# A retention layer and a gated convolution on one core: the lead-in in a new order and on other banks, the loads of the loop issued later

## The chip, the core and the metric

The kernel runs on one core of a Trainium2 chip. The core has a matrix engine (TensorE, "PE" in the profile, with its weight loads as "PEld"), VectorE ("DVE"), ScalarE ("ACT"), GpSimd ("POOL") and a queue engine (SyncE, "SP") that issues most DMAs. Each engine takes its instructions strictly in the order of the program and waits at semaphores for the others. The metric is the device time of one execution in microseconds (us).

## What is computed

For 8 sequences of 576 rows with 8 heads of 64, a causal retention (scores with a decay per head, no softmax) is followed by a gated linear unit whose gate is a causal convolution of 5 taps:

```python
scores = (q @ k.T) / sqrt(64)
ret    = scores * gamma[h] ** (row - col)   # 0 where col > row
x      = ret @ v                            # heads side by side: [8, 576, 512]
gate   = sigmoid(sum_k conv_w[k] * x shifted by 4 - k rows)
out    = ((gate * (x @ w_val)) @ w_out)     # float32, [8, 576, 512]
```

Inputs and output are float32; the kernel multiplies in bfloat16.

## The kernel before

**Units.** A unit is 256 rows of one sequence (two 128-row chunks), so units 0 to 15 are the two halves of the eight sequences. Units 16 and 17 hold the last 64 rows of four sequences each. The order of work on every engine is written out by hand (`tc.manual_schedule()`), unit by unit, and Tile only adds the semaphores.

**What happens to a unit.** `load_half` (L104) brings half the heads of k, q or v, 256 KB, over the SP queue (L113); units 0, 1, 16 and 17 are loaded whole, the last two in four pieces per tensor (L97). Many loads have a *touch*: a one-element copy on DVE or ACT into the tile (L112), for which the DMA waits, so the touch's place in that engine's order sets when the DMA goes out. `cast1` and `cast_half` (L256, L274) convert to bf16; v is always converted on POOL (L264, L282), k and q on POOL or another engine. `turn` (L296) or, in the loop, `turn_halves` (L306) transposes k and q on PE, and `take_part` (L321) or L319 copies the result to `kqt`. `scores` multiplies them, `masks` (L346) applies the causal mask on DVE. `values` multiplies the masked scores with v into the banks `o0` and `o1`; `carried` adds the contribution of earlier rows from a running state to the same banks. `update` multiplies k with v, ACT copies the product to `xf` (L453, L455) and `states` (L464) adds it to the state on POOL. `take_x` (L414) scales the result on DVE into `xg`. Then `conv` and `gates` (the sigmoid on ACT, L527), `value` and `gated` (DVE, L547), and `project` with its copy on ACT (L562) and `store`.

**Order.** The stretch from the start to about 43 us, here called the lead-in, is a list of such calls without a loop: it takes units 0 to 3, loads the weights, and leaves every unit at its place in the pipeline. The loop `for n in range(4, NU)` (L770) then runs 14 turns. Turn n does `carried`, the second half of `scores`, and `values` of unit n, `conv`, `value` and `project` of unit n-1, and `update`, `turn_halves` and casts of the units ahead. POOL gets in turn n, in this order: the states of unit n+1, v of n+2, the second halves of k and q of n+2, and the first halves of k and q of n+3; the transposes that need these first halves stand in turn n+1.

**Banks.** PSUM has the pools `ps_a` (one tile of two banks), `ps_s` (one of two), `ps_o` (`o0`, `o1`) and `ps_v` (two tiles of one bank). A new tile waits for the last reader of the old one in its place.

**Fillers.** `warm(n, cols)` multiplies a zero tile. `fill()` (L151) adds zero products until the count of matmuls at the start of the loop has the remainder 50 modulo 127.

```python
def load_half(n, u, i, touch=None):
    ...
    if touch:
        touch(t[0:1, 0, 0:1], lsc[0:1])
    nc.sync.dma_start(out=t, in_=...)
```

All matmuls and transposes are recorded under L146, so groups of PE are told apart by their tiles.

Of the kernel before, what the change touches and what calls it, by code (L numbers as in the profile page):

```python
# [21 lines left out]
def kernel(  # L22
# [10 lines left out]
    nc = tc.nc  # L33
# [44 lines left out]
    with tc.manual_schedule():  # L78
# [72 lines left out]
        def fill():  # L151
            z = ps_v.tile([P, 512], F32, name="v")
            while (made[0] + 4 * NP) % BLOCK != PLACE:
                matmul(z[:, 0:64], lhsT=zero[:, 0:P], rhs=zero[:, 0:64], start=True, stop=True)
# [80 lines left out]
        def prep_wv(e, eng):  # L235
            for (j0, ab, hl) in (((0, 0, 0), (64, 0, 1)), ((0, 1, 1), (64, 1, 0)))[e]:
                for pr in range(2):
                    eng(wvb[e][:, :, pr, j0:j0 + 64], wvf[2 * pr + ab][:, :, hl * 64:hl * 64 + 64])

        def prep_wo(os, eng):  # L240
            for o in os:
                if o < 2:
                    eng(wob[:, o, :], wof[o])  # L243
                else:
                    eng(wob[lo, o, :], wof[o][hi])
                    eng(wob[hi, o, :], wof[o][lo])

# [57 lines left out]

        def turn_halves(*pairs):  # L306
            if len(pairs) == 1:
                ps = ps_v.tile([P, 1, 2, 2, 2, P], BF16, name="v")
            else:
                ps = ps_a.tile([P, 2, 2, 2, 2, P], BF16, name="a")  # L310
            for (at, (u, hf)) in enumerate(pairs):
                for i in range(2):
                    for prl in range(2):
                        for r in range(2):
                            h = 2 * (2 * hf + prl)
                            transpose(ps[:, at, i, prl, r, :], bf[u]["kq"[i]][:, r, h:h + 2, :].rearrange("p h d -> p (h d)"), ident)
            for (at, (u, hf)) in enumerate(pairs):
                new_turned(u)
                nc.scalar.copy(kqt[u][hf].rearrange("p i l r c a -> p (i l r c a)"), ps[:, at].rearrange("p i l r a -> p (i l r a)"))  # L319

        def take_part(u, i, eng):  # L321
            for hf in range(2):
                eng(kqt[u][hf][:, i].rearrange("p l r c a -> p (l r c a)"),  # L323
                    tps[u, i][:, hf].rearrange("p l r a -> p (l r a)"))
# [49 lines left out]
        def carried(u, odd, chs=(0, 1)):  # L374

            kind, b, cu = units[u]
            o = out_banks(u)
            for pr in range(NP):
                t = kqt[u][pr // 2]
                for c in chs:  # L380
                    par = c ^ odd
# [16 lines left out]
        def fence(u, rows, c, eng=None):  # L398
            t = small.tile([P, 1], F32, name="fence", bufs=2)
            (eng or nc.scalar.copy)(t[rows], ops[u][c][rows, NP - 1, 0:1])  # L400

        def values(u, hf):
# [29 lines left out]

        def update(u, own=False, now=True):
            kind, b, cu = units[u]
# [3 lines left out]
            if own:  # L438
                xy = [ps_v.tile([P, 512], F32, name="v") for c in range(2)]
            else:  # L440
                xyt = ps_s.tile([P, 2, 512], F32, name="s")
                xy = [xyt[:, c] for c in range(2)]
# [20 lines left out]

        def states(u):  # L464
            kind, b, cu = units[u]
# [10 lines left out]
            else:  # L476
                mid = stp.tile([P, NP, 64], F32, name="mid")
                nc.gpsimd.tensor_tensor(mid, state[b, "run"], xf[:, 0], op=ALU.add)  # L478
                nc.gpsimd.tensor_copy(s1, mid)
                s2 = stp.tile([P, NP, 64], BF16, name=f"s4{b}", bufs=1)  # L480
                nc.gpsimd.tensor_tensor(s2, mid, xf[:, 1], op=ALU.add)
            state[b, 2 * cu + 1] = s1
            state[b, 2 * cu + 2] = s2

# [60 lines left out]
        def gated(j, i, e):  # L545
            ss = sets(j, i)
            nc.vector.tensor_tensor(zsb[j][:, 2 * e + ss[0]:2 * e + ss[-1] + 1, :], gsb[j, i][e], vps[j, i, e], op=ALU.mult)  # L547
# [81 lines left out]
        warm(2)  # L629
        update(0, own=True)  # L630
        cast1("q", 1, act)
        cast1("v", 1)
        values(0, 0)
        warm(1, 512, ps_s)
        values(0, 1)
        fence(0, lo, 1, dve)
        turn(1, ps_v, 0)
        take_part(1, 0, act)
        take_x(0, (0,))
        carried(0, 1)  # L640
        carried(0, 0)
        turn(1, ps_v, 1)
        take_x(0, (1,))
        take_part(1, 1, dve)
        conv(0, 0)
        load_wv(1, act)
        load_wv(3)
        carried(1, 1, (0,))
        carried(1, 0, (0,))
        scores(1, 0)  # L650
        masks(1, 0)
        load_half("k", 3, 0, dve)
        scores(1, 1, pool=ps_a)
        masks(1, 1)
        load_half("k", 3, 1, dve)
        cast1("k", 2)
        update(1, own=True)
        cast1("q", 2, act)
        load_half("q", 3, 0, act)
        cast1("v", 2)  # L660
        values(1, 0)
        turn(2, ps_v, 0)
        take_part(2, 0, act)
        warm(1, 512, ps_s)
        values(1, 1)
        take_x(1, (0,))
        fence(1, lo, 1, dve)
        load_half("q", 3, 1, dve)
        warm(2, 512, ps_s)
        turn(2, ps_v, 1)  # L670
        take_part(2, 1, dve)
        load_half("v", 3, 0, dve)
        carried(1, 1, (1,))
        carried(1, 0, (1,))
        take_x(1, (1,))
        load_half("v", 3, 1, dve)
        warm(1, 512, ps_s)
        scores(2, 0)
        masks(2, 0)
        load_wo(0, dve)  # L680
        load_wo(1)
        scores(2, 1, pool=ps_v)
        masks(2, 1)
        load_wo(2, dve)
        load_wo(3)
        prep_wv(0, pool)
        prep_wv(1, act)
        conv(1, 0)
        update(2)
        cast1("k", 3)  # L690
        values(2, 0)
        values(2, 1)
        take_x(2, (0,))
        fence(2, lo, 1, dve)
        load_half("k", 4, 0, dve)
        value(0, 0, 0)
        carried(2, 1)
        carried(2, 0)
        take_x(2, (1,))
        load_half("k", 4, 1, dve)  # L700
        gated(0, 0, 0)
        load_half("q", 4, 0, dve)
        gate_values(0, 1)
        load_half("q", 4, 1, dve)
        cast1("v", 3)
        cast1("q", 3, act)
        conv(2, 0)
        gate_values(1, 0)
        load_half("v", 4, 0, dve)
        load_half("v", 4, 1)  # L710
        gate_values(1, 1)
        load_half("k", 5, 0, dve)
        load_half("q", 5, 0)
        turn(3, ps_o, 0)
        take_part(3, 0, act)
        turn(3, ps_o, 1)
        take_part(3, 1, dve)
        update(3, now=False)
        states(3)
        prep_wo((0, 1), pool)  # L720
        prep_wo((2, 3), act)
        cast1("k", 4)
        gate_values(2, 0)
        load_half("v", 5, 0, dve)
        load_half("v", 5, 1)
        gate_values(2, 1)
        cast1("q", 4, act)
        cast1("v", 4)
        scores(3, 0)
        masks(3, 0)  # L730
        load_half("k", 5, 1, dve)
        load_half("q", 5, 1)
        carried(3, 0)
        scores(3, 1, lambda: carried(3, 1), pool=ps_a)
        masks(3, 1)
        load_half("k", 6, 0, dve)
        load_half("q", 6, 0)
        project(0, 0, 0, 4)
        project(0, 0, 1, 4)
        store(0)  # L740
        turn_halves((4, 0))
        project(1, 0, 0, 4)
        values(3, 1)
        values(3, 0)
        cast_half("k", 5, 0)
        cast_half("q", 5, 0)
        update(4)
        take_x(3)
        load_half("v", 6, 0, dve)
        load_half("v", 6, 1)  # L750
        turn_halves((4, 1), (5, 0))
        project(1, 0, 1, 4)
        store(1)
        scores(4, 0)
        masks(4, 0)
        prep_tail_mask()
        load_half("k", 6, 1, dve)
        load_half("q", 6, 1)
        cast1("v", 5)
# [4 lines left out]
        fill()  # L764
        project(2, 0, 0, 4)
        project(2, 0, 1, 4)
        store(2)
        load_half("k", 7, 0)
        load_half("q", 7, 0)
        for n in range(4, NU):  # L770
# [8 lines left out]
            conv(n - 1, 0)  # L779
            bring("v", n + 3, 0, act)  # L780
            if nxt:
                scores(n + 1, 0, pool=ps_v)
                masks(n + 1, 0)
                update(n + 1)
            bring("v", n + 3, 1, act)
            values(n, 1)
            values(n, 0)
            gate_values(n - 1, 0)
            bring("k", n + 3, 1, dve)
            gate_values(n - 1, 1)  # L790
            bring("q", n + 3, 1, dve)
            take_x(n, (0,))
            take_x(n, (1,))
            bring("k", n + 4, 0, dve)
            if n + 2 < NU:
# [6 lines left out]
            if nxt:  # L802
                turn_halves((n + 1, 1), *([(n + 2, 0)] if n + 2 < NU else []))
            bring("q", n + 4, 0, act)
            project(n - 1, 0, 0, 2)
# [36 lines left out]
```

## Time and profile before

| | |
|---|---|
| runs shown | 159.75, 160.12, 162.49 us (median 160.12) |
| the profiled execution | 159.02 us, span of the trace 157.3 us |
| granted TensorE clock | 0.999 |
| busy: PE, PEld | 145.8 us (93%), 115.3 us |
| busy: DVE, ACT, POOL | 105.2, 93.4, 102.4 us |
| moved by DMA | 40.37 MB, mean 257 GB/s |
| chain that ended last | PE 80%, DVE 8%, DMA 3%, ACT 2% |

The span is the time from the first to the last instruction of the program; the execution's own time is 1.7 us longer. In the timeline's rows, the first number is the start, the second the duration of the group, "xN" the number of instructions, and the bracket tells how long the engine stood idle before the group and who ended that. Matmuls overlap in the records, so the cost of a group of matmuls is read from its start to the start of the next one.

### The profile page before, as it was taken

To read this page: it belongs to the slowest core of one execution; us is meant where nothing else is said; L and a number is where in the kernel's file an instruction comes from. 1 tells how busy PE (TensorE), PEld (TensorE's weight loads), DVE (VectorE), ACT (ScalarE), POOL (GpSimd) and SP (SyncE) were. 2 spreads that over 40 slices of the span, in tenths; PEclk is the share of its full clock that TensorE was granted. 3 is DMA by queue.
4 is the path that set the end of the run, shared out by engine and by line. 5 is a ranking of instruction groups with operands and counts; after the bars stand their busy time and mean duration, and the time that the engine had idled before them with its cause. 6 is when DMAs were issued, how large, how long until landed. Compare 5 with 4: busy or idle time off the path is not lost.

```text
span 157.3 us, 8008 instructions
## 1 busy us (share of the span) xinstructions
PE 145.8 (93%) x3461; PEld 115.3 (73%) x3461; DVE 105.2 (67%) x214; ACT 93.4 (59%) x164; POOL 102.4 (65%) x166
## 2 busy tenths in 40 slices
PE   6977989989999999999999999999999999998960
PEld 2456667868788878877878788887878887876720
DVE  5786887693676867667768686767667676765340
ACT  6895664697846574747484848484656637252510
POOL 7679669397969695959596877869695842500000
PEclk9999999999999999999999999999999999999999
DMA  4999999999989999998999899899778872302135
GB/s 117 347 347 342 324 290 333 325 310 308 351 276 292 300 352 363 321 315 234 305 264 314 249 322 285 262 314 267 213 230 241 262 236 108 137 17 121 36 101 133
DMA packets 62561, 40.37 MB, mean 257 GB/s; under 512 B 2346, under 2 KB 59710, under 8 KB 62526
## 3 DMA queue, kind: packets, MB, share of 16 engines
q1 hardware_dynamic: 62400, 39.59, 82.1%
q8 instruction: 27, 0.44, 1.2%
q10 hardware_dynamic: 126, 0.27, 0.7%
q14 instruction: 8, 0.07, 0.1%
HBM read 30.42 MB, written 9.44 MB: 253 GB/s over the span
## 4 chain that ended last, share of the span: by engine, by line
PE 80%; DVE 8%; DMA 3%; ACT 2%; issue 1%; SPq 1%; POOL 1%; POOLq 0%; DVEq 0%
PE v L146 45%; PE a L146 19%; PE o L146 10%; PE s L146 7%; DVE p L356 3%; DMA fv<-in_v_dram 2%; DVE p L352 2%; SPq L586 1%; DMA out_dram<-ob 1%; DVE z L547 1%; DVE kq L323 1%; ACT ob L562 1%; POOL wob L243 1%; DVE xg L421 1%; ACT gate L527 1%
## 5 line engine op out<-in xcount | busy, mean ns | idle before, releaser
L319 ACT COPY kq<-a 128x1024 bf16<-128x1024 bf16 x26 | 25.0, 1015 | 28.0 <-PE a L146 28.0
L146 PE MATMUL v<-xg,wvb 128*128 128x256 bf16 x288 | 34.8, 273 | 0.3
L146 PE MATMUL v<-wob,z 128*128 128x256 bf16 (+1 forms) x209 | 32.9, 305 | 1.2 <-POOL wob L243 0.6
L547 DVE TENSOR_TENSOR z<-gate,v 128x512 bf16<-128x512 f32 x34 | 23.3, 686 | 14.0 <-PE v L146 11.5
L356 DVE TENSOR_TENSOR p<-s,mask 128x1024 bf16<-128x1024 f32 x17 | 20.8, 1223 | 17.1 <-PE s L146 17.1
L146 PEld LDWEIGHTS <-wvb 128*128 128x128 bf16 x288 | 26.7, 97 | 5.2 <-issue 0.2
L264 POOL TENSOR_TENSOR vb<-fv,gin 128x512 bf16<-128x512 f32 x28 | 28.6, 1042 | 0.0
L146 PEld LDWEIGHTS <-z 128*128 128x128 bf16 x217 | 20.3, 98 | 9.2 <-issue 1.7
L421 DVE TENSOR_TENSOR xg<-o,gout 128x512 bf16<-128x512 f32 x32 | 22.3, 736 | 4.5 <-PE o L146 4.4
L527 ACT ACTIVATE gate<-a 128x1024 f32<-128x1024 f32 x17 | 17.4, 1024 | 12.6 <-ACT ob L562 6.7
L146 PE MATMUL a<-xg,dg 64*64 64x256 bf16 x720 | 24.3, 270 | 0.6 <-DVE xg L421 0.3
L562 ACT COPY ob<-v 128x512 f32<-128x512 f32 x34 | 18.6, 581 | 5.1 <-PE v L146 5.1
L146 PEld LDWEIGHTS <-dg 64*64 64x64 bf16 x720 | 20.0, 106 | 1.4 <-issue 0.7
L146 PEld LDWEIGHTS <-kb 64*64 64x64 bf16 (+1 forms) x656 | 15.9, 107 | 5.0 <-DVE p L356 2.0
L271 POOL CAST kb<-fk 128x512 bf16<-128x512 f32 x28 | 17.0, 612 | 0.1
L146 PEld LDWEIGHTS <-kq 64*64 64x64 bf16 x576 | 15.6, 106 | 2.0 <-issue 1.7
L352 DVE TENSOR_TENSOR p<-v,mask 128x512 bf16<-128x512 f32 x24 | 15.4, 685 | 1.0
L478 POOL TENSOR_TENSOR mid<-run,xf 128x256 f32<-128x256 f32 x8 | 5.8, 726 | 13.5 <-ACT xf L455 12.3
L271 POOL CAST qb<-fq 128x512 bf16<-128x512 f32 x22 | 13.5, 614 | 0.1
L146 PE MATMUL o<-p,vb 64*64 64x128 bf16 x576 | 12.3, 218 | 0.9 <-DVE p L356 0.5
L146 PEld LDWEIGHTS <-s 64*64 64x64 bf16 x256 | 8.2, 107 | 6.2 <-issue 3.4
L146 PE MATMUL s<-kq 64*64 64x128 bf16 x304 | 12.2, 222 | 0.4 <-DVE kq L323 0.3
(98 smaller groups left out, 197.2 us busy)
## 6 DMA issues: line engine op xcount, KB each, us to landing
out_dram<-ob SPq DMA_DIRECT2D x16, 512.0 KB, 4.5
fk<-in_k_dram SPq DMA_DIRECT2D x28, 256.0 KB, 4.5
fq<-in_q_dram SPq DMA_DIRECT2D x28, 256.0 KB, 4.6
fv<-in_v_dram SPq DMA_DIRECT2D x28, 256.0 KB, 4.6
wkc<-in_k_dram SPq DMA_DIRECT2D x2, 512.0 KB, 5.0
wqc<-in_q_dram SPq DMA_DIRECT2D x2, 512.0 KB, 5.5
wvc<-in_v_dram SPq DMA_DIRECT2D x2, 512.0 KB, 5.9
wvf<-in_moe_w_val_dram SPq DMA_DIRECT2D x4, 256.0 KB, 4.9
```

The lines of the kernel that those rows point to most:

```text
L146: return f(*a, **k)
L243: eng(wob[:, o, :], wof[o])
L264: nc.gpsimd.tensor_tensor(b[n][:, hs].rearrange("p h r d -> p (h r) d"), f.rearrange("p h (r d) -> p (h r) d", r=2), gin[:, units[u][2], h ...
L271: (eng or nc.gpsimd.tensor_copy)(b[n][:, :, hs].rearrange("p r h d -> p h r d"), f.rearrange("p h (r d) -> p h r d", r=2))
L319: nc.scalar.copy(kqt[u][hf].rearrange("p i l r c a -> p (i l r c a)"), ps[:, at].rearrange("p i l r a -> p (i l r a)"))
L352: nc.vector.tensor_tensor(p[:, par].rearrange("p l r a -> p l (r a)"), sps[u, hf][par].rearrange("p l r a -> p l (r a)"), mrow.to_broadcas ...
L356: nc.vector.tensor_tensor(p.rearrange("p e l r a -> p (e l) (r a)"), sps[u, hf].rearrange("p e l r a -> p (e l) (r a)"), mrow.to_broadcast ...
L421: nc.vector.tensor_tensor(x[:, b, :, PAD + i0:PAD + i0 + P].rearrange("p o (a r) -> p o r a", r=2), o[c].rearrange("p o (r a) -> p o r a", ...
L478: nc.gpsimd.tensor_tensor(mid, state[b, "run"], xf[:, 0], op=ALU.add)
L527: nc.scalar.activation(t, cps[j, i], AF.Sigmoid)
L547: nc.vector.tensor_tensor(zsb[j][:, 2 * e + ss[0]:2 * e + ss[-1] + 1, :], gsb[j, i][e], vps[j, i, e], op=ALU.mult)
L562: (eng or nc.scalar.copy)(outs[u][:, r], o)
```

## The change

The lead-in's list of calls is rewritten from the first `update` to the loop, some calls go to other banks and engines, and in the loop every load stands three transfers later. In detail:

- `update(0)` takes `ps_s` in place of two tiles of `ps_v`, `update(1)` also `ps_s`, `update(3)` and `update(4)` take `ps_o`. `scores(1, 1)` takes `ps_v` in place of `ps_a`.
- `turn_both(3, ...)` puts the transposes of k and q of unit 3 into one tile of `ps_s`, ahead of both copies. `conv(0)` and `conv(1)` have their `gates` later in the order.
- The copies of the turned k parts of units 1 and 2 go from ACT to DVE, the q part of unit 1 from DVE to ACT; the casts of k and q of unit 3 and of parts of others go to ACT.
- `fence_zero(1)` and `fence_first(3)` are one-column DVE reads of the bank just written by `carried`, which `values` then waits for. `carried` runs its heads and chunks backwards.
- `states` can be cut in two (`states_last`).
- Of the zero products, `warm` of 64 columns x12 comes in, three calls of `warm` with 512 columns go out, and `fill()` aims at the same remainder with one `project` left behind it.
- In the loop, turn n loads the second halves of k and q of unit n+2, the first halves of k and q of n+3 and both halves of v of n+3; before, v of n+3, the second halves of n+3, and the first halves of n+4.

```diff
-            while (made[0] + 4 * NP) % BLOCK != PLACE:
+            while (made[0] + 8) % BLOCK != PLACE:
...
         def prep_wv(e, eng):
-            for (j0, ab, hl) in (((0, 0, 0), (64, 0, 1)), ((0, 1, 1), (64, 1, 0)))[e]:
-                for pr in range(2):
-                    eng(wvb[e][:, :, pr, j0:j0 + 64], wvf[2 * pr + ab][:, :, hl * 64:hl * 64 + 64])
+            for pr in range(2):
+                if e == 0:
+                    eng(wvb[e][:, :, pr, :], wvf[2 * pr])
+                else:
+                    for i in range(2):
+                        eng(wvb[e][:, :, pr, i * 64:i * 64 + 64], wvf[2 * pr + 1][:, :, 64 - i * 64:128 - i * 64])
...
+        def turn_both(u, engs):
+            new_turned(u)
+            ps = ps_s.tile([P, 2, 2, 2, 2, P], BF16, name="s")
...
+            for i in range(2):
+                take_part(u, i, engs[i])
...
-            for pr in range(NP):
+            for pr in reversed(range(NP)):
...
-                for c in chs:
+                for c in reversed(chs):
...
+        def fence_zero(u):
+            t = small.tile([P, 1], F32, name="fence", bufs=2)
+            nc.vector.tensor_copy(t[hi], ops[u][0][hi, 0, 32:33])
...
+        def states_last(u):
+            kind, b, cu = units[u]
+            s2 = stp.tile([P, NP, 64], BF16, name=f"s4{b}", bufs=1)
+            nc.gpsimd.tensor_tensor(s2, state[b, "mid"], xfs[u][:, 1], op=ALU.add)
```

The new order of the lead-in, from the first update on (calls of one line follow each other; loads are left out except where a touch is named):

```python
update(0); values(0, 0); turn(1, ps_v, 0); cast1("q", 1, act); cast1("v", 1)
warm(1, 512, ps_s); values(0, 1); take_part(1, 0, dve); fence(0, lo, 1, dve); take_x(0, (0,))
turn(1, ps_v, 1); carried(0, 1); carried(0, 0); take_part(1, 1, act); take_x(0, (1,)); warm(12, 64, ps_s)
scores(1, 0); masks(1, 0); scores(1, 1, pool=ps_v); masks(1, 1); conv(0, 0, False)
carried(1, 1, (0,)); carried(1, 0, (0,)); fence_zero(1); cast1("k", 2); cast_half("q", 2, 0, act)
update(1, now=False); states(1, False); cast_half("q", 2, 1, act); gates(0, 0)
values(1, 0); turn(2, ps_v, 0); values(1, 1); fence(1, lo, 1, dve); take_part(2, 0, dve); take_x(1, (0,))
load_half("k", 3, 0, dve); turn(2, ps_v, 1); take_part(2, 1, dve); carried(1, 1, (1,)); carried(1, 0, (1,))
take_x(1, (1,)); cast1("v", 2); states_last(1); scores(2, 0); masks(2, 0); scores(2, 1, pool=ps_v); masks(2, 1)
prep_wv(0, act); conv(1, 0, False); update(2, now=False); gates(1, 0); prep_wv(1, pool)
values(2, 0); value(0, 0, 0); gated(0, 0, 0); values(2, 1); fence(2, lo, 1, dve); take_x(2, (0,)); states(2)
value(0, 0, 1); gated(0, 0, 1); carried(2, 1); carried(2, 0); take_x(2, (1,))
cast1("k", 3, act); cast1("q", 3, act); cast1("v", 3)
value(1, 0, 0); gated(1, 0, 0); value(1, 0, 1); gated(1, 0, 1); turn_both(3, (act, dve)); conv(2, 0)
prep_wo((0, 1), pool); scores(3, 0); masks(3, 0); value(2, 0, 0); gated(2, 0, 0); update(3, ps_o, False)
prep_wo((2, 3), act); states(3, False); value(2, 0, 1); gated(2, 0, 1); scores(3, 1, pool=ps_a); masks(3, 1)
project(0, 0, 0, 4); carried(3, 1); carried(3, 0); fence_first(3); states_last(3); cast1("k", 4)
cast_half("q", 4, 0, act); project(0, 0, 1, 4); store(0); cast_half("q", 4, 1, act); cast1("v", 4)
values(3, 1); values(3, 0); take_x(3); prep_tail_mask(); project(1, 0, 0, 4); turn_halves((4, 0), pool=ps_a)
project(1, 0, 1, 4); store(1); cast_half("k", 5, 0); cast_half("q", 5, 0, act); project(2, 0, 0, 4)
scores(4, 0); masks(4, 0); update(4, ps_o); turn_halves((4, 1), (5, 0)); cast1("v", 5)
cast_half("k", 5, 1); cast_half("q", 5, 1); cast_half("k", 6, 0); cast_half("q", 6, 0)
fill(); project(2, 0, 1, 4); store(2)
```

And the loads in the loop:

```diff
             conv(n - 1, 0)
-            bring("v", n + 3, 0, act)
+            bring("k", n + 2, 1, act)
...
                 update(n + 1)
-            bring("v", n + 3, 1, act)
+            bring("q", n + 2, 1, act)
...
             gate_values(n - 1, 0)
-            bring("k", n + 3, 1, dve)
+            bring("k", n + 3, 0, dve)
             gate_values(n - 1, 1)
-            bring("q", n + 3, 1, dve)
+            bring("q", n + 3, 0, dve)
             take_x(n, (0,))
             take_x(n, (1,))
-            bring("k", n + 4, 0, dve)
+            bring("v", n + 3, 0, dve)
...
-            bring("q", n + 4, 0, act)
+            bring("v", n + 3, 1, act)
```

## The prediction

> **What bounds the kernel now.** I read the page's busy slices first, then the table by stage with the loop's turns as stages, then PE's timeline of the lead-in, and last SP's and POOL's timelines at the end of the loop.
>
> ```profile
> PE   6977989989999999999999999999999999998960
> DMA  4999999999989999998999899899778872302135
> ...
> 57.69:65.00 7.31, 7.29 (x190) 6.10 (x192) 5.31 (x10) 4.62 (x10) 5.64 (x10) 1.00 1.10 346
> 117.60:124.92 7.32, 7.30 (x190) 6.12 (x192) 5.19 (x7) 4.53 (x9) 5.13 (x8) 1.00 0.86 249
> 124.92:132.36 7.44, 7.28 (x167) 6.07 (x169) 5.20 (x7) 3.93 (x6) 2.60 (x5) 1.00 0.66 220
> ```
>
> The slices and the turns (stretch, length, then busy time of PE, PEld, DVE, ACT, POOL, clock, DMA share, GB/s) show a loop bound by PE: 7.29 of 7.31 us busy, at full clock. An order of loads can't shorten such a turn; it can only lengthen it. A gain can come only from the lead-in.
>
> ```profile
> 15.69 0.42 PE L146 MATMUL a<-kq 64*64 64x128 bf16 x16 [0.65 <-ACT gate L527]
> 17.97 0.60 PE L146 MATMUL s<-zero 128*128 128x512 bf16 x2
> 19.75 0.42 PE L146 MATMUL s<-kq 64*64 64x128 bf16 x16
> 33.53 0.38 PE L146 MATMUL v<-wob,z 128*128 128x256 bf16 x2 [0.39 <-POOL wob L243]
> 40.48 0.41 PE L146 MATMUL v<-zero 128*128 128x64 bf16 x8
> 42.80 0.24 PE L146 MATMUL o<-kq,s 64*64 64x128 bf16 x1
> ```
>
> These are PE's rows from the lead-in: waits, zero products, and the loop's start at 42.80. From the first update (9.88) that is 32.9 us. Its useful products, start to start: 5 updates of 0.36, 8 half values of 0.33, 6 turns of 0.44, 3 half turns of 0.45, 48 carried products of 0.044, 3 conv of 1.14, 7 half scores of 0.30, 6 value of 0.93, 6 project of 0.94 make 27.3. So 5.6 us are waits and zeros: 1.9 are the zeros at 10.48, 17.31, 17.97, 19.30 and 40.48, the rest waits.
>
> **Part 1, the new lead-in.** It computes the same 27.3 us. I lay the new order on each engine with durations from rows and list where PE waits.
>
> - Start: update(0) writes the bank that the mask of 8.70 reads for 1.23, so 9.93: 0.05. Then one zero product of 512 columns, 0.21.
> - Turn of q 1: ACT ends its cast of k 1 at 10.36; the copy of update(0) starts 0.55 after that product, 10.48 to 11.0; the cast of q 1 takes 1.06, to 12.04. PE is free at 11.60: 0.44.
> - scores(1,0): the q copy goes to ACT, 12.04+0.66+1.05=13.75. PE is through with carried and the 12 small zeros (0.32) at 13.15: 0.60.
> - values(1,0) must wait for fence_zero, and that stands behind both masks on DVE: scores end 14.22, masks 1.15+1.20 to 16.57, fence 0.15, 16.72. PE is free at 16.20: 0.52.
> - scores(2,0): before, ACT copied k 2 at 18.11 while DVE did take_x. Now DVE alone does fence, k copy, take_x, touch and q copy:
>
> ```profile
> 18.08 0.76 DVE L421 TENSOR_TENSOR xg<-o,gout 128x512 bf16<-128x512 f32 x1 [0.51 <-PE o L146]
> 19.13 0.76 DVE L323 COPY kq<-v 128x512 bf16<-128x512 bf16 x2 [0.21 <-PE v L146]
> ```
>
> values(1,1) starts 17.49, so 17.49+0.47+0.07+0.68+0.65+0.06+0.76=20.18. PE is free at 18.61: 1.57, the largest new wait. Behind it on DVE come take_x and masks of unit 2; two stops of 0.06 follow.
> - PE then runs 11.7 us of products to 31.97 and meets the first project. Its weights stand on ACT behind the gates of conv(2) (starts 28.01, +1.34, 1.02) and the copies of update(3), which start 30.93 and take 0.54; four casts of 0.62, row L245, end at 33.95. PE stops 0.28 and 1.00 inside that project.
>
> The sum is 5.1 against 5.6: the loop starts 8.1 us of products after 34.20, at 42.27, **0.5 earlier**. The loads of unit 3 now wait for later touches on DVE (k 3 issued 19.5 against 17.20), so v 3 lands about 26.5 by 0.735 us per 256 KB (queue full); update(3) asks for it at 30.4. This cover is 1.9 us wide after the casts; it costs nothing.
>
> **Part 2, turn 4.** Update(4) moves from 37.9 to 40.1. POOL stands waiting for its copy, with v 5, k 5 and q 5 queued behind the states: ACT copies it at 40.71 to 41.25, states 1.5, so v 5 from 42.55 (before: 40.66), 2.0, k 5 to 45.17. Update(5) asks at 44.5 and stops 0.67. On ACT the two copies of turn_halves (0.92, 1.00) end at 43.17 and free `ps_a`; conv(3) asks at 42.86: 0.31. Turn 4 is **1.0 longer**. The other turns are not: the casts on POOL start 5.3 us into a turn, as now, and the transposes want them in the next turn.
>
> **Part 3, the loads in the loop.** Full units have room: q of n+3 is touched 5.4 us into the turn (the place of 48.20), lands 3.2 to 5.4 later, is cast in 0.61, so at most 11.4; the transposes want it at 7.4+5.2=12.6. The tail units have not. Each tensor takes four issues on SP:
>
> ```profile
> 109.44 2.98 SPq L97 DMA_DIRECT2D wkc<-in_k_dram  x4
> 112.85 2.95 SPq L97 DMA_DIRECT2D wqc<-in_q_dram  x4
> 116.39 2.26 SPq L97 DMA_DIRECT2D wvc<-in_v_dram  x4
> 118.74 2.75 SPq L97 DMA_DIRECT2D wkc<-in_k_dram  x4
> 121.60 1.89 SPq L97 DMA_DIRECT2D wqc<-in_q_dram  x4
> 124.08 3.96 SPq L97 DMA_DIRECT2D wvc<-in_v_dram  x4
> ...
> 126.29 0.61 POOL L271 CAST kb<-wkc 128x512 bf16<-128x512 f32 x1
> 127.81 0.61 POOL L271 CAST qb<-wqc 128x512 bf16<-128x512 f32 x1 [0.91 <-DMA wqc<-in_q_dram]
> ...
> 130.24 0.39 PE L146 MATMUL a<-ident,qb 128*128 128x128 bf16 x4
> ```
>
> POOL already waits 0.91 for q 17, at 127.81; PE wants it at 130.24, a cover of 1.8. Now k 16 is touched behind gated(12,0), at 114.95 and not 109.4. On the clock of before and by the mean of these six rows (2.80): k 16 to 117.75, q 16 to 120.55, v 16 to 123.35, a store 0.4, k 17 (touched 122.2) to 126.55, q 17 to 129.35, its last piece issued 128.9. The last pieces of the four k and q rows landed 3.2, 2.8, 4.3 and 4.5 us after their issue, mean 3.7: 132.6, cast to 133.2, **3.0 late** (some 1.6 of it already at q 16 in turn 14). POOL runs its orders strictly, so states, v 16 and the rest queue behind these casts; their users come a turn later. Bounds: with no pause in the issue (1.89 per four) and 2.8 to land nothing is late, 0; with 5.0, the longest of these landings, 4.3. I take 3.0, from the rows of the same transfers.
>
> [...]
>
> **Sum.** -0.5+1.0+3.0=+3.5 us. On the profiled execution's 159.02 (span 157.3 and 1.7 around it) that is 162.5; the median of the runs shown is 1.1 above it, so I give 160.12+3.5=163.6.
>
> **Rivals.**
> - *The tail lands in time* (not slower). If the pauses in the issue (0.4 is an undisturbed piece, some take 1.6 to 2.5) fall elsewhere, k 16 goes out 114.95 to 116.84, q 16 to 118.73, q 17 122.2 to 126.0 and lands 128.4, cast by 129.0, before 130.24. For it: the 1.89 row. Against: five of six rows are slower. It decides when both q land before 122.2 and 129.6. Time: 160.12+0.5=160.6.
> - *The lead-in gains more* (faster). If DVE and ACT pass their two chains without holding PE, 1.57 and 1.28 fall away, and with turn 4 and the tail at nothing the sum is -3.4: 156.7. For it: the two chains lie on engines busy 6 to 8 tenths there. Against: each chain is in order, with measured durations.
> - *Every turn waits for its loads* (much slower). A pause of 1.6 to 2.5 on the queue, seen on SP at 44.41 and 49.88 too, uses up the 1.2 us that q of n+3 has. If half of the ten turns 4 to 13 lose 0.8, it is 163.6+4.0=167.6. Against: landings of 3.0 to 5.4 in the loop.
> - *A load isn't later*: where SP stands behind a store anyway, the touch doesn't set the issue. That is so for v 16 only, and is in the sum.
>
> **How the numbers follow.** Forecast 0.50 (own range 161.8 to 165.0, as the tail goes from 1.2 to 4.3 with the lead-in's error), tail in time 0.20, faster 0.10, every turn 0.20. A measurement of this kernel can tell about 2%, 3.2 us, from no change: the bound above is 163.3. Of the forecast's 0.50, 0.30 lie above it, with the last rival 0.50 slower; 0.40 within; 0.10 faster. The range 160.4 to 166.4 leaves out the faster case and half of the slowest.
>
> **What would show it.** Right: turn_halves of units 16 and 17 idle on PE until POOL's q casts, POOL waiting for DMA there; scores of unit 2 idle about 1.5 us behind DVE; the first project behind ACT's `wob`; update of unit 5 behind POOL; loop start near 42.3. Wrong: PE without gaps in turns 14 and 15, or POOL waiting for loads in every turn, or a loop start off by over 1.5 us.

## The result, and the profile after

The changed kernel takes 168.69 us (median of four runs, 166.47 to 170.56); the kernel before took 160.44 beside it. The ratio is 1.042, with a 95% interval of 1.031 to 1.053: slower by more than the 2% that can be told apart. The forecast was 163.6 with a range up to 166.4, so the sign was right and the size was not. Medians here are over all runs of a kernel, and the ratios leave out runs over 1.5% above that kernel's fastest. The profiled execution of the changed kernel took 168.15 us (span 166.4, against 157.3 before).

First the page of the changed kernel: PE's busy slices, the engines' shares of the chain that ended last, and two groups (busy, mean ns, then idle time ahead of them and what ended it).

```profile
PE   6978789779899799999989999999399998999860
...
PE 70%; DVE 7%; DMA 6%; issue 6%; ACT 3%; SPq 2%; POOL 2%; POOLq 0%; DVEq 0%; ACTq 0%
...
L146 PEld LDWEIGHTS <-kb 64*64 64x64 bf16 (+1 forms) x656 | 16.1, 106 | 9.6 <-issue 4.9
...
L146 PE MATMUL s<-vb,kb 64*64 64x64 bf16 x448 | 7.2, 196 | 5.3 <-issue 4.3
```

A slice of the loop now holds a 3 where all were 9. "issue" has 6% of the chain against 1% before: PE stood, and no engine and no transfer that the profile knows ended the wait. The two groups say where: ahead of the products of `update`, s<-vb,kb, 4.3 us. Next four turns of the loop by stage (stretch, length, busy PE, PEld, DVE, ACT, POOL, clock, DMA share, GB/s).

```profile
52.81:61.32 8.51, 7.48 (x202) 6.14 (x195) 5.30 (x10) 4.49 (x10) 6.52 (x11) 1.00 0.86 264
114.70:126.49 11.79, 9.10 (x203) 6.95 (x196) 5.32 (x10) 4.55 (x9) 6.47 (x11) 0.86 0.68 201
126.49:133.96 7.47, 7.39 (x206) 6.26 (x200) 5.34 (x10) 4.56 (x7) 3.87 (x6) 1.00 0.84 245
133.96:142.08 8.12, 7.53 (x194) 6.21 (x189) 5.18 (x7) 4.06 (x6) 4.48 (x6) 1.00 0.77 229
```

A turn without trouble (14, at 126.49) lasts 7.47 us as before. Turn 5 (52.81) has lost 1.2, and turn 13 (114.70) 4.3, at a granted clock of 0.86. Turn 15 (133.96), where the loads of the tail units should have cost most, has lost only 0.55. PE's timeline shows the worst stand (a time in which PE stood still), and the stages behind it the clock:

```profile
116.33 0.44 PE L146 MATMUL s<-vb,kb 64*64 64x64 bf16 x30
119.38 0.22 PE L146 MATMUL s<-vb,kb 64*64 64x64 bf16 x2 [2.61 <-issue]
```

```profile
119.38:121.00 1.62, 1.62 (x39) 1.20 (x40) 0.00 (x0) 0.67 (x2) 0.66 (x2) 0.63 0.65 186
121.00:122.50 1.50, 1.50 (x9) 1.07 (x8) 0.42 (x1) 0.00 (x0) 1.44 (x3) 0.50 0.51 152
```

PE stopped inside a run of 32 equal products, two products before its end, for 2.61 us. Then the clock was 0.50, and PE was busy 9.10 us in that turn for what takes 7.4: the stand cost 2.6 and its aftermath 1.7.

**What PE stood for.** The trace has a DMA queue of kind "instruction" with 27 packets of 16 KB, one for every 256 instructions of PE (the pages list 3461 weight loads, each has its product, and 9 and 19 others come on top in the two kernels). I counted PE's instructions (weight loads, products, and waits that are instructions of their own) in the two traces and in those of the 17 experiments below, in the loop's stretch from weight load 900 to 2800. There are 42 gaps of over 0.6 us from one weight load to the next, and all 42 lie at instruction 192 or 193 modulo 256. I read these as borders of blocks of code, at which PE stands because the next block hasn't come: behind each of the 42 it goes on 1.1 to 1.6 us after the packet has moved. In the loop a packet moves only after PE has passed the border before, and mostly takes 0.9 to 1.2 us. The shortest blocks of the loop last 3.8 to 4.1 us in the two kernels, and 38 of the 42 gaps lie at the end of such a short block. For the stand above, PE passed a border at 112.5, the packet moved from 115.60 to 118.21 (it took 2.61, the longest of all), and PE went on at 119.38.

**The two traces, term by term**, in the profiled executions (us; the third column is experiment e13 below, the changed kernel without one wait in the loop; one execution each):

| | forecast | changed kernel | e13 |
|---|---|---|---|
| start of the loop's first conv, against 43.17 | -0.2 | +2.2 | +1.9 |
| length of turn 4 | +0.7 | 0 | 0 |
| turns 5 to 13 | 0 | +6.4 | -0.6 |
| turns 14 and 15 | +3.0 | +0.6 | +2.5 |
| span, against 157.3 | +3.5 | +9.1 | +3.7 |

(The forecast's 1.0 for turn 4 had 0.31 ahead of that conv and 0.67 behind it. The rows are differences of the starts of the loop's convs.)

### The profile page after: what moved, and what is told of

Its sections match the earlier page's. It is cut to its first block, busy times and chain, and to the rows that moved or that the text cites. A ratio compares the mean times of both kernels' runs of the same rounds, so it can differ in the third digit from the quotient of the medians.

```text
span 166.4 us, 7990 instructions
## 1 busy us (share of the span) xinstructions
PE 146.6 (88%) x3445; PEld 115.5 (69%) x3461; DVE 105.3 (63%) x219; ACT 93.7 (56%) x161; POOL 102.1 (61%) x163
## 4 chain that ended last, share of the span: by engine, by line
PE 70%; DVE 7%; DMA 6%; issue 6%; ACT 3%; SPq 2%; POOL 2%; POOLq 0%; DVEq 0%; ACTq 0%
PE v L146 37%; PE a L146 16%; PE o L146 10%; PE s L146 7%; DMA fk<-in_k_dram 5%; SPq L97 2%; DMA wqc<-in_q_dram 2%; DVE z L581 1%; ACT wob L249 1%; DVE p L372 1%; DVE xg L447 1%; DVE kq L339 1%; POOL vb L267 1%; ACT qb L290 1%; DVE p L368 0%
## 5 line engine op out<-in xcount | busy, mean ns | idle before, releaser
L335 ACT COPY kq<-a 128x1024 bf16<-128x1024 bf16 x27 | 26.1, 1015 | 30.6 <-PE a L146 30.6
L146 PE MATMUL v<-xg,wvb 128*128 128x256 bf16 x288 | 36.6, 280 | 0.7 <-issue 0.4
L146 PEld LDWEIGHTS <-wvb 128*128 128x128 bf16 x288 | 27.4, 100 | 6.4 <-issue 1.0
L274 POOL CAST kb<-fk 128x512 bf16<-128x512 f32 x26 | 15.8, 614 | 4.3 <-DMA fk<-in_k_dram 4.0
L368 DVE TENSOR_TENSOR p<-v,mask 128x512 bf16<-128x512 f32 x26 | 16.7, 684 | 1.5 <-PE v L146 0.5
L274 POOL CAST qb<-fq 128x512 bf16<-128x512 f32 x21 | 12.9, 616 | 2.4 <-DMA fq<-in_q_dram 0.7
L146 PE MATMUL s<-vb,kb 64*64 64x64 bf16 x448 | 7.2, 196 | 5.3 <-issue 4.3
```

The source lines that it names most:

```text
L146: return f(*a, **k)
L274: (eng or nc.gpsimd.tensor_copy)(b[n][:, :, hs].rearrange("p r h d -> p h r d"), f.rearrange("p h (r d) -> p h r d", r=2))
L368: nc.vector.tensor_tensor(p[:, par].rearrange("p l r a -> p l (r a)"), sps[u, hf][par].rearrange("p l r a -> p l (r a)"), mrow.to_broadcas ...
```

## The experiments

### Which part of the change costs

**e1**, the kernel before with the changed loads of the loop. Each load stands four transfers later in the order, not three: v of n+3 goes from the first place of a turn to the fifth. The four loads ahead of the loop that this replaces are left out.

```diff
             conv(n - 1, 0)
-            bring("v", n + 3, 0, act)
+            bring("k", n + 2, 1, act)
...
-            bring("k", n + 4, 0, dve)
+            bring("v", n + 3, 0, dve)
```

> The kernel before with only the loop's loads changed: turn n loads k and q (second halves) of unit n+2, k and q (first halves) and v of n+3, and the four transfers that stood ahead of the loop for this (k 6 and q 6 second halves, k 7 and q 7 first halves) are left to it. Theory A (code blocks: in the changed kernel PE stands 0.6 to 2.8 us, by 'issue', at every place that is a multiple of 127.7 weight loads on, because the 16 KB of its next instructions come late behind the loads; the loads' new order does it): 164 to 167 us, with issue waits in the loop of 3 us or more. Theory B (the new lead-in does it, through the backlog that it leaves, or by its own waits): 160.4 plus at most the lateness of the tail loads, 0.5 to 3, no issue waits in the loop beyond the 0.5 of the kernel before.

Measured: 162.25 us, ratio 1.013 (1.002 to 1.025).

**e2**, the changed kernel with the old loads of the loop (these lines the other way round, and the four loads ahead of the loop):

```diff
-            bring("k", n + 2, 1, act)
+            bring("v", n + 3, 0, act)
...
-            bring("v", n + 3, 0, dve)
+            bring("k", n + 4, 0, dve)
```

> The changed kernel with the loop's loads as before; the four transfers stand ahead of the loop again. Theory A (the loads' new order makes the code late): the loop costs what it cost before, and only the lead-in's +2.2 us is left: 162 to 163.5. Theory B (the lead-in does it): 166 to 169 us, with PE's issue waits in the loop as in the changed kernel.

Measured: 167.26 us, ratio 1.050 (1.038 to 1.061).

**e4**, the changed kernel with the loads of units 16 and 17 alone at their old places:

```diff
-                if u < NU:
+                if u < NU - 2:
                     load_half(name, u, i, eng)
...
+            bring_tail("k", n + 4, dve)
```

> The changed kernel with the loads of units 16 and 17 alone back at their places of before (k and q one turn earlier, v at the front of the turn). The prediction's theory of the tail: k 16 to q 17 were the 3.0 us term, so -3 us and no DMA wait of POOL in turns 13 to 15. By the trace of the changed kernel PE waited only 0.4 us for POOL there: -0.4 to -0.6 us. Theory A: the other waits, by issue, stay.

Measured: 169.64 us, ratio 1.064 (1.054 to 1.075), not below the changed kernel.

What follows: the late loads are worth some 2 us where nothing else stands in front of them (e1, whose interval reaches from 0.3 to 4 us), and nothing in the changed kernel. The large loss comes with the new lead-in, although it shows in the loop. The only part of that edit that also reorders the loop's PE work is `carried`, which runs its heads and chunks backwards.

### The order of `carried`

**e3**, the kernel before with eight zero products fewer ahead of the loop, which puts every border of code eight products later in the work:

```diff
-        BLOCK, PLACE = 127, 50
+        BLOCK, PLACE = 127, 42
```

> The kernel before with the remainder 42 in place of 50 at the start of the loop: the eight zero products of the filler go out, and every border between two blocks of PE's instructions falls 8 products later in the work. Counted on the trace of before, the shortest stretch of work that covers a block falls from 4.24 to 3.2 us (five of them in the loop). If the next block's code takes some 3.9 us from the border to its use (1.6 until it moves, 0.95 to move, 1.3 more), PE stands about 0.7 us at five to six borders: +2 to +5 us. If the borders cost nothing: -0.5 us, the eight zeros.

Measured: 161.46 us, ratio 1.004 (0.998 to 1.010). A shift of the borders alone does nothing, though it makes the shortest blocks 2.5 to 3.1 us long.

**e5**, the kernel before with `carried` as the change has it:

```diff
-            for pr in range(NP):
+            for pr in reversed(range(NP)):
...
-                for c in chs:
+                for c in reversed(chs):
```

> The kernel before with one part of the change alone: the carried products run backwards over heads and chunks, in the lead-in and in the loop. It is the only part of the new lead-in that also changes PE's order inside the loop: with it the first carried weight load of a turn waits for DVE and POOL at once, and the trace of the changed kernel shows one wait instruction more on PE in every turn (11 of them). Theory B1 (that wait, or the borders of code that the added instructions move, makes the code late in the loop): 164 to 167 us, issue waits of 3 us or more. Theory B2 (what the lead-in leaves behind: where engines and queue stand when the loop starts): 160.4 within 1 us, as before.

Measured: 165.89 us median, 162.68 to 168.87; the runs differ too much among themselves for a ratio. Two reversed loops cost about 5 us by the median, and 1.7 in the fastest run.

**e6** and **e7**, the kernel of e2 and the changed kernel with `carried` in its old order in the units of the loop:

```diff
-            for pr in reversed(range(NP)):
+            for pr in (range(NP) if u >= 4 else reversed(range(NP))):
...
-                for c in reversed(chs):
+                for c in (chs if u >= 4 else reversed(chs)):
```

> The kernel of the run with the new lead-in and the old loads (167.3 us), with the carried products of the loop's units in the order of before. Theory B1: the loop is as before, and only the lead-in's 2 us stay: 162 to 163.5. Theory B2: 166 to 168, issue waits unchanged.

> The changed kernel with the carried products of the loop's units in the order of before. Theory B1: 2 us of the lead-in and some 1.5 to 2 of the later loads (measured on the old lead-in) stay: 163.5 to 165. Theory B2: 167 to 169.

Measured: 163.07 (ratio 1.013, 1.003 to 1.022) and 164.90 (1.022, 1.014 to 1.030). The old order in the loop takes off 4.2 and 3.8 us. The difference of the two, 1.8, fits the late loads again, though their intervals overlap.

**e8**, the changed kernel without the stores of turns 5 to 15:

```diff
-            store(n - 1)
+            if n in (4, NU - 2, NU - 1):
+                store(n - 1)
```

> The changed kernel without the stores of the loop's turns 5 to 15: 5.8 of 9.4 MB of output are not written. If the blocks of PE's code come late because they queue behind the data on the DMA engines, a fifth less of data in the loop lets them pass: PE's issue waits in the loop (4.6 us) fall under 1 us, 163 us. If a block is late for a reason on PE's side, the waits stay: 167 to 169.

Measured: 166.10 us, ratio 1.023 (1.012 to 1.033). Two of the stands remain in its trace (1.43 and 1.15 us from one product to the next). Less traffic seems to help a little (1.023 against 1.042, though the intervals overlap).

### The order, or the wait that it makes

The stream of PE's instructions shows what the backward order does to the first product of a turn. The changed kernel, then the kernel before:

```
2000 L146 Ldweights s_1482 [waits DVE_49,Pool_49]
2001 L146 Matmult o_1606<-kq_1325,s_1482 64x128 [waits Activation_49]

2000 L146 Ldweights s_1251
2001 L146 Matmult o_1618<-kq_1278,s_1251 64x128 [waits DVE_49]
2002 L146 Ldweights s_1495 [waits Pool_49]
```

The backward order begins with the state that POOL made last and with the half of kq that ACT copied last, into a bank that DVE has just read. These are three waits for two instructions. One of them becomes an instruction of its own on PE's sequencer, in each of eleven turns; the loop before had none.

**e9**, the kernel before with that wait and nearly the old order (the diff), and **e10**, the kernel before with (0, 3, 2, 1) in place of (3, 0, 1, 2): nearly the whole backward order and no such wait:

```diff
-            for pr in range(NP):
+            for pr in (3, 0, 1, 2):
...
-                for c in chs:
+                for c in reversed(chs):
```

> The kernel before, carried taking the chunks in reverse and the pairs of heads as 3, 0, 1, 2, so that of the backward order little is left but its first product, and that first weight load of every turn again waits for DVE and POOL at once. Theory W (the second wait, an instruction of its own on PE's sequencer in each turn, is what delays the blocks of code): as slow as the kernel with the whole order reversed, 164 to 167 us, and stands without a releaser of 1 us or more at loads near 1500, 1883 and 2649. Theory O (the order of the products themselves: other banks read first by take_x, other rows of PE): nearly the old order, 160.3 to 162 us. Theory D (it is only that the borders of the code blocks drift ahead, one instruction a turn): as W here, and told apart by the run with seven zero products more.

> The kernel before, carried taking the chunks in reverse and the pairs as 0, 3, 2, 1: nearly the whole backward order, but the first weight load of a turn waits for POOL alone and the first product for DVE, so no second wait stands in the stream. Theory W: 160.3 to 162 us, as the kernel before, with borders of code 128 loads apart. Theory O: 164 to 167 us. Theory D: as W.

Measured: e9 167.87 us median (164.36 to 172.21, too uneven for a ratio), e10 162.87 (ratio 1.017, 1.008 to 1.026). By the medians the wait without the order costs 7.3 us and the order without the wait 2.3; e9's size is uncertain, but its fastest run (164.36) is slower than e10's slowest (163.56). Theory O falls as the main cause; the 2 us of e10 are more than theory W gives. Its trace holds one stand of 1.9 us with half a clock behind it, although the loop has no wait of this kind.

**e11**, the kernel before with seven zero products more, so that the borders come about as much earlier as the added instructions push them:

```diff
-        BLOCK, PLACE = 127, 50
+        BLOCK, PLACE = 127, 57
```

> The kernel before with seven zero products more ahead of the loop, so that every border of a block of code in the loop falls seven products earlier in the work, about as far as the eleven added waits push it by the last turn; no wait is added. Theory W: 160.5 to 162 us (the zeros themselves are 0.2 us). Theory D: 163.5 us or more, with stands of over 1 us at the borders of the odd turns.

Measured: 160.98 us, ratio 1.006 (1.001 to 1.010). Theory D falls.

**e13**, the changed kernel with the pairs of the loop as 0, 3, 2, 1, so that the wait goes and the order stays nearly backward:

```diff
-            for pr in reversed(range(NP)):
+            for pr in ((0, 3, 2, 1) if u >= 4 else reversed(range(NP))):
```

> The changed kernel, with the loop's carried taking the pairs as 0, 3, 2, 1 and the chunks in reverse as the change has it, so that its first weight load waits for POOL alone. Theory W (the second wait in each turn delays the code): as the changed kernel with the old order in the loop or up to the 2 us more that this order cost on the kernel before, 164.5 to 167 us, and no stand of 2 us without a releaser. Theory O (the order): 168.5 to 170 us.

Measured: 163.75 us; the kernel before took 159.60 beside it, ratio 1.026 (1.019 to 1.032) against 1.042 for the changed kernel. PE's waits by what ended them (sum in us, times, longest), in the changed kernel and then in e13:

```profile
PE s L146 <- issue: 4.3, 3, 2.6
...
PE v L146 <- issue: 0.7, 2, 0.4
...
PE a L146 <- issue: 0.6, 1, 0.6
```

```profile
PE a L146 <- issue: 0.6, 1, 0.6
```

The 0.7 is 0.32 in turn 8 and 0.38 in the lead-in. What is left in e13 is one stand of the lead-in; the loop has none. Its turns, by stage:

```profile
52.50:59.85 7.35, 7.27 (x203) 6.05 (x196) 5.31 (x10) 4.40 (x10) 6.24 (x11) 1.00 0.97 301
111.79:119.14 7.35, 7.27 (x204) 6.05 (x197) 5.33 (x10) 4.46 (x9) 5.45 (x10) 1.00 0.86 268
127.52:136.65 9.13, 7.53 (x195) 6.20 (x189) 5.17 (x7) 4.06 (x6) 4.49 (x6) 1.00 0.72 214
```

Turn 13 (111.79) takes 7.35 in place of 11.79 with the same products. Turn 15 (127.52) now shows the late loads, which hardly show in the changed kernel. This execution is the fastest of e13's four (162.72 against a median of 163.75), so the others may hold a stand.

### Where the wait must stand, and what traffic does

**e15** and **e16**, the order of e9 in the odd units from 5 on alone, and in the even units from 6 on alone (`u % 2 == 0` in the first line):

```diff
+            back = u >= 5 and u % 2 == 1
-            for pr in range(NP):
+            for pr in ((3, 0, 1, 2) if back else range(NP)):
...
-                for c in chs:
+                for c in (chs[::-1] if back else chs):
```

> The kernel before with the second wait in the odd units from 5 on alone (six of the eleven turns). There the wait stands 11 weight loads behind a border of code, at the start of the shortest block (4.1 to 4.2 us). Theory P (the wait delays the request for the block whose border is just behind PE): 164 to 168 us, nearly the whole cost. Theory E (a wait costs the same in any turn): 163 to 165 us. Theory N (waits cost only when every turn has one): 160.5 to 162 us.

> The kernel before with the second wait in the even units from 6 on alone (five of the eleven turns), where it stands 79 weight loads behind a border. Theory P: 160.5 to 162 us, as the kernel before. Theory E: 163 to 164.5 us, five elevenths to the same sum as in the odd turns. Theory N: 160.5 to 162 us, and told apart by the odd turns.

Measured: e15 165.19 us, ratio 1.030 (1.021 to 1.039); e16 159.72, ratio 1.0005 (0.997 to 1.004). Six waits some ten weight loads behind a border carry the cost, five waits nearly 80 behind one cost nothing: theory P. PE's waits of 0.3 us or more that ended in "issue", in e15 and then in e16:

```profile
PE s L146 <- issue: 4.0, 3, 2.1
```

```profile
PE o L146 <- issue: 0.5, 1, 0.5
PE s L146 <- issue: 0.3, 1, 0.3
```

The times of the packets agree. This is the time from PE's passing the border at the head of the short block to the move of the next packet, at weight loads near 990, 1374, 1757, 2141 and 2524, worked out from the trace (us, one execution each):

| kernel | wait | five delays | mean |
|---|---|---|---|
| before | none | 0.95, 2.28, 0.46, 0.50, 0.40 | 0.9 |
| e13 | none | 0.23, 0.34, 0.33, 0.73, 0.72 | 0.5 |
| e16 | even turns | 1.89, 1.20, 0.22, 1.00, 2.10 | 1.3 |
| e15 | odd turns | 1.29, 2.71, 2.71, 0.22, 3.90 | 2.2 |
| changed | all | 2.82, 1.54, 2.68, 0.46, 3.08 | 2.1 |
| e9 | all | 3.10, 2.69, 3.69, 0.92, 2.71 | 2.6 |

A short block lasts 4.1 us, a transfer about 1.0, and PE stands where the transfer ends less than 1.1 to 1.6 us before the next border. From these numbers (4.1 less 1.0, less 1.1 to 1.6) I estimate that a delay of up to 1.5 or 2 us is nearly free and that what lies above it is paid; in the kernel before, the delay of 2.28 went with a stand of 0.28. But the groups overlap: e11 and e6, without the wait, have means of 2.1 and 1.9 and are little slower. By the count of gaps over 0.6 us in that stretch, the eight kernels with the wait in the odd turns have 2 to 5 each, the eleven others 0 to 2. So code comes late without the wait too (a gap of 2.1 us in e10, 1.9 in e1 and e17); with it, this happens more often.

**e14**, the kernel of e9 with the loads of v left out for units 8 to 15:

```diff
+            if n == "v" and 8 <= u < NU - 2:
+                loaded[n, u] = loaded[n, 7]
+                return
```

> The kernel before with the second wait in every turn (chunks in reverse, pairs 3, 0, 1, 2: 167.87 us), and the loads of v left out for units 8 to 15, whose casts read the tiles of unit 7; a third of the loop's loads are gone. Theory T (the blocks of code come late because they stand behind data in the DMA engines, which the loop keeps about 90% busy; where the DMA engines are idle, at the end of the program, they move 0.4 to 0.8 us after the border, in the loop 0.7 to 4.1): 159 to 162 us, and delays of about 1 us. Theory S (PE's sequencer, held at the wait, asks for the next block too late; traffic has nothing to do with it): 165 to 168 us, and delays of 3 us as before.

Measured: 165.14 us, ratio 1.025 (1.015 to 1.035). With the DMA engines at a share of 0.71 in place of 0.87 (stage 45 to 130) the mean of the five delays is 2.4, hardly less than e9's 2.6, and stands remain. Theory T falls as the whole cause and S is nearer. Traffic may still matter: at the program's end, with the DMA engines mostly idle, the last three packets move 0.2 to 0.8 us after the border in every kernel; but no wait of this kind stands there either.

### The lead-in

**e12**, the kernel of e6 with ACT's casts of wob ahead of update(3), and **e17**, that kernel with a value projection ahead of scores(3, 0):

```diff
+        prep_wo((2, 3), act)
         value(2, 0, 0)
         gated(2, 0, 0)
         update(3, ps_o, False)
-        prep_wo((2, 3), act)
```

> The changed kernel with the old loads of the loop and the loop's carried in its old order (163.07 us when it ran), and ACT's casts of the last two rows of wob issued ahead of update of unit 3 instead of behind it. If the wait of the first project for those casts is a real part of the lead-in's 1.4 to 2 us, as the sum had it (1.28 us named, 1.15 us of idle measured): 0.8 to 1.1 us less than that kernel, 162.0 to 162.3 us, loop start earlier by as much. If the wait only moves on (to the loop start, where POOL's state for the carried of unit 4 and ACT's kq are 0.2 us behind PE): 162.7 us or more, and the loop starts within 0.4 us of where it did.

```diff
+        value(2, 0, 0)
         scores(3, 0)
         masks(3, 0)
...
-        value(2, 0, 0)
```

> The changed kernel with the old loads of the loop, the loop's carried in its old order, the casts of wob early (161.76 us when it ran, ratio to the kernel before 1.005), and one more wait of the lead-in filled: the projection of unit 2's first value group issued ahead of the first scores of unit 3, where PE idled 0.88 us for ACT's and DVE's copies of the turned k and q. If that idle was on the path: 0.5 to 0.9 us less, 159.5 to 160.3 us against a kernel before of 159.6 to 160.5, so the new lead-in is then worth what the old one is, and does not beat it by what can be measured. If it is not on the path: a ratio of 1.005 again.

Measured: e12 161.76 us, ratio 1.005 (1.000 to 1.010), against 1.013 (1.003 to 1.022) for e6: the intervals overlap. The first conv of the loop starts at 44.37 in place of 44.52. The wait for wob is gone from the trace, and a wait of 0.84 us has come right behind its place, behind POOL's state of unit 3. e17: 161.16, ratio 1.007 (1.002 to 1.011), that conv at 43.93. So these waits mostly move on, and no version here beats the kernel before.

## Why the prediction was wrong where it was

**The step that failed is "The other turns are not [longer]."** It rested on the loads alone. The order of `carried` was read as a matter of banks, and in Part 1 its products were priced unchanged, 0.044 each, which is right. That its first weight load would bring one wait more as an instruction of its own, and that this wait would stand some ten weight loads behind a border of code, in the turns with the shortest block, was not in the sum. It costs 4 to 5 us by the medians (e5, e6, e7), and 6.4 in the profiled turns 5 to 13: 4.6 of stands, 1.7 of half clock. The page before held a hint: "issue" ahead of weight loads, and a stand of 0.28 us at the same kind of border.

**The sum without that step holds as a total, not in its parts.** e13's span is 3.7 us over the one before, and the forecast said 3.5. That they agree is luck: the lead-in was 2.1 worse than forecast, and turn 4, turns 5 to 13 and the tail were 1.8 better together.

- *Lead-in*, forecast -0.5 at the loop's start (42.27), measured 44.41. PE's waits there:

```profile
15.62 0.62 PE L146 MATMUL a<-xg,dg 64*64 64x256 bf16 x13 [0.58 <-issue]
19.99 0.42 PE L146 MATMUL s<-kq 64*64 64x128 bf16 x16 [0.83 <-DVE kq L339]
25.00 0.72 PE L146 MATMUL v<-xg,wvb 128*128 128x256 bf16 x5 [0.38 <-issue]
30.92 0.42 PE L146 MATMUL s<-kq 64*64 64x128 bf16 x16 [0.88 <-DVE fv L112]
34.77 0.38 PE L146 MATMUL v<-wob,z 128*128 128x256 bf16 x2 [0.21 <-ACT wob L249]
36.04 0.38 PE L146 MATMUL v<-wob,z 128*128 128x256 bf16 x2 [0.89 <-ACT wob L249]
44.41 0.21 PE L146 MATMUL o<-kq,s 64*64 64x128 bf16 x1 [0.23 <-ACT kq L335]
```

The wait for wob is as forecast (0.28 and 1.00 against 0.21 and 0.89), and that of scores(2, 0) is there and half as long (1.57 against 0.83), since PE came later. What the list lacked: two late blocks of code (0.58, 0.38), scores(3, 0) behind ACT's and DVE's copies of the turned k and q (0.88; the row names the touch right behind DVE's copy), and the loop's first product (0.23). Together they are 2.07. Against them, the waits forecast ahead of scores(1, 0) and values(1, 0) (0.60 and 0.52) did not come, and others were shorter. In all PE is idle for 4.54 us of the 34.43 from its first update to the loop, against 2.80 of 32.92 before: 1.7 more, where the sum had 0.9 more (3.7 to 4.6). And its busy time fell only from 30.12 to 29.89, although 1.4 us of zero products were to go. These two make most of the 2.14 missed; where the gain of the zeros went, no run here shows. A bound of over 1.5 us on the loop start was named as what would prove the working wrong, and it was passed.

- *Turn 4*, forecast 1.0: 0.27 ahead of conv(3) came as forecast (0.31). The stop of update(5) behind POOL came as 0.3 in place of 0.67: its second half starts at 47.07, right behind POOL's cast of k 5 (47.01). PE was 2.1 later there than laid out, and POOL 1.8. The turn was no longer than before.
- *The tail*, forecast 3.0 us of waits: e13 has 0.74 and 1.38, and its two turns are 2.5 longer. Right in place and mechanism, somewhat too large. In the changed kernel POOL waits as forecast, yet PE hardly does (POOL's rows, then PE's):

```profile
127.53 0.62 POOL L274 CAST kb<-wkc 128x512 bf16<-128x512 f32 x1 [2.52 <-DMA wkc<-in_k_dram]
130.64 0.62 POOL L274 CAST qb<-wqc 128x512 bf16<-128x512 f32 x1 [2.49 <-DMA wqc<-in_q_dram]
...
138.65 0.62 POOL L274 CAST qb<-wqc 128x512 bf16<-128x512 f32 x1 [1.36 <-DMA wqc<-in_q_dram]
```

```profile
139.33 0.40 PE L146 MATMUL a<-ident,qb 128*128 128x128 bf16 x4 [0.37 <-POOL qb L274]
```

PE had lost 4.3 us in turn 13. The loads issued before it landed meanwhile (the DMA engines' share falls to 0.16 at 122.50 to 124.00), and the eight pieces of k 16 and q 16 then went out in 4.0 us (from 122.85), against 5.0 in e13 (from 116.17). That the stand caused this is argued, not shown. It fits e4, which takes the late tail loads back and gains nothing.

**The rivals.** "Every turn waits for its loads" gave 167.6, close to the result, and is false as a mechanism: POOL waits for loads in turns 5 to 13 of e13 too, and these turns last 7.35 to 7.47 us. "The lead-in gains more" failed on the waits above. "The tail lands in time" nearly holds for the changed kernel, behind a stand that the forecast did not have, and fails in e13.

**What stays open.** That the wait carries most of it and that its place decides is shown by e13, e15 and e16. What the order alone adds in e15's odd turns is not known: no run has it there without the wait, and the interval of e10 (1.008 to 1.026) overlaps e15's. Nor is it known how PE's sequencer, held at the wait, comes to get its next block later: in e15 one packet (turn 11) moved 0.8 us before its turn's wait was released, and that turn's delay is short in all kernels of the table. e10's single stand has no cause here either.

## What to carry to other kernels

Before reordering products, look at which engines the first instruction of the new order waits for, and begin with an operand that has been ready longest. Here a first weight load that waited for DVE and POOL brought PE one wait instruction more per turn; six of those took e15 to a ratio of 1.030, and without them e13 had no stand left in the loop. When PE stands with nothing to release it, count instructions from such a stand to the next. In these traces all 42 gaps lay at instruction 192 or 193 modulo 256, one packet of code apart or several; and the waits that brought the stands of e15 stood some ten weight loads behind the border before, not at the stand. And price a stall once: behind the stand of 2.61 us the late loads of this kernel hardly showed (+0.6 us in turns 14 and 15, against +2.5 in e13), and undoing those of the tail gained nothing (e4).

## What the runs showed of the hardware

- The trace shows packets of 16 KB on the instruction queue, 27 in each of the two kernels, one for every 256 instructions of PE. In the loop the next one moves only once PE has passed the border before, 0.22 to 3.90 us later in the table of delays, and mostly takes 0.9 to 1.2 us. In the kernel before, one border of the loop shows a stand, of 0.28 us. Where a block lasts only 4 us, one border cost up to 2.61 us of standing in the changed kernel, and 2.9 in e2.
- Behind some stands of PE of about 2 us the granted clock was near half, behind others it was full. The mean over the 3.2 us behind the stand was 0.61 after 1.9 us (e9), 0.53 after 2.1 (e10), 0.60 after 2.3 (e15) and 0.57 after 2.8 (the changed kernel), stands taken from product to product. It was 1.00 after stands of 2.0 and 3.1 in e2 and of 2.1 and 2.3 in e4. What decides between the two, no run here shows.
